# A recurrent attention layer with a token mixer behind it: k and r loaded four tokens to a partition, states kept as diagonal blocks, the last batch's V loaded whole, and a new order of steps

## The chip, the core and the metric

One core of a Trainium2 chip runs the whole program. The time is that of the device for one execution, in microseconds, as the median of several runs. Beside the runs there is one profiled execution with its trace: its span is the time from the first to the last instruction. The engines are TensorE (PE, with its weight loads PEld), VectorE (DVE), ScalarE (ACT), GpSimd (POOL) and SyncE (SP), which here only issues DMA transfers.

## The reference

Inputs r, k, v and w are float32 of the shape (4 batches, 8 heads, 768 tokens, 48 values); u is (8, 48). Each batch and head runs a recurrence over the tokens; the outcome of all heads side by side (384 values a token) then goes through a mixer over the tokens.

```python
for t in range(S):
    cur = np.einsum('bhd,bhe->bhde', u[None] * kt, vt)
    y[:, :, t] = np.einsum('bhd,bhde->bhe', rt, state + cur)
    state = wt[:, :, :, None] * state + np.einsum('bhd,bhe->bhde', kt, vt)
...
wq = x @ w_q                       # (tokens, 64)
wk = x @ w_k
W_tok = scale * np.einsum('bsd,btd->bst', wq, wk)
mixed = np.einsum('bst,btd->bsd', W_tok, x)
return np.maximum(mixed, 0.0) @ w_out
```

## The kernel before

The work is cut into 12 units of 256 tokens (three to a batch), each of two chunks of 128 tokens. For a unit, `unit` (L406) lays out these steps:

- Load w, k, r, v (`load`, L229): each partition takes two neighbouring tokens of every head, so a row is 96 floats (384 bytes), and all 128 partitions are filled by one transfer. In seven units (`DIRECT`, L339) V is loaded by `load_v` (L221) in four transfers of 64 partitions and 192-byte rows, which put the tokens into their order at once. In the other five V is put in order on PE by a permutation matrix (`f_v16` L565, `f_vp` L570) and copied out of PSUM (`f_vb` L580). There are four buffers for each of w, k, r and v.
- ACT takes the logarithm of w (lw, L466), POOL, ACT or DVE cast k and r to bf16 (`f_c16`, L472). PE sums the logarithms with a mask CM (`f_cw`, L485), ACT makes the exponentials en and ep (L497, L503). PE transposes k and r (`f_rawT`, L510). DVE or ACT copies kT (ks), DVE makes RT = rT x ep and qT = rT x ks, POOL or DVE makes KT = ks x en (L545). POOL makes ptm (L552), the decay over a chunk, by head.
- PE multiplies KT and RT (`f_A` L608, 64-row tiles), DVE masks it with US (AM, L618, 128x1024).
- PE transposes KT back (kb), ACT or DVE copies it with a scale (kd). The state: `f_sn` (L650) adds the old state through the identity (384 columns) and four products of 128 by 96 columns, each for a pair of heads, of which DVE keeps the diagonal blocks by a product with ptm, zero elsewhere (`f_sb` L664, SB of 384 columns).
- y: eight products with AM and four of the old state with RT (`f_y`, L673). DVE adds the bonus term Vd from POOL (X, L704).
- For the mixer PE transposes X (xt), a copy makes XT, PE makes wk and wq (`f_qk`, L728), a copy makes QK. When the three units of a batch are done: T (`f_T` L766, six products of 384 columns), TS, and for each unit mx, rl (relu, MX), fp (product with wo), os (copy) and a store. The order of tokens is undone in the operand of `f_mx` (L793).

Pieces of the last unit are cut in halves (`each`) to shorten the end. Every product is issued through `mm` (L181), so the profile has all of PE's work on that line.

The order on each engine is decided before the kernel is built. `Plan.add` records a step with its engine, length and a rank; `Plan.order` (L64) sorts each engine's queue by rank and walks through them with the buffers' ring sizes and PSUM's eight banks, issuing the step that can start first. `RANK` (L304) holds the ranks, `ENG` the engine for steps that may run on either of two. SyncE's queue is such a queue: loads and stores follow each other in it. The setup ahead of unit 0 (L245 to L293) clears buffers on DVE and builds masks on POOL; 42 products with a zero matrix (`warm`, L385) and nine at the start keep PE running.

Of the kernel before, what the change touches and what calls it, by code (L numbers as in the profile page):

```python
# [14 lines left out]
AX = mybir.AxisListType  # L15
# [9 lines left out]

class Plan:

    def __init__(self, kinds, switch):
        self.kinds = kinds
        self.switch = switch
        self.steps = []

    def add(self, eng, dur, rank, fn, after=(), fill=None, read=(), lag=100, mode=0,
            behind=None):
        s = dict(mode=mode, behind=behind, eng=eng, dur=dur, rank=rank, fn=fn, after=[a for a in after if a is not None],  # L40
                 fill=fill, lag=lag, n=len(self.steps), out=[])
        s["buf"] = None if fill is None else dict(readers=[])
        self.steps.append(s)
        for a in read:
            self.reads(s, a)
        return s

    def dma(self, issue, dur, rank, fn, after=(), fill=None, read=()):

        i = self.add("SP", issue, rank, fn, after, fill, read, lag=0)  # L50
        m = self.add("DQ", dur, 0, self.nothing, [i], lag=0)
        return i, self.add(f"L{m['n']}", 1950, 0, self.nothing, [m], lag=0)

    def nothing(self):
        pass

    def reads(self, s, a, own=False):

        if not own:
            s["after"].append(a)  # L60
        if a["buf"] is not None:
            a["buf"]["readers"].append(s)

    def order(self):  # L64
        never = 1 << 60
        queues = {e: [] for e in ("PE", "ACT", "DVE", "POOL", "SP")}
        for s in sorted(self.steps, key=lambda s: s["rank"]):
            if s["eng"] in queues:
                queues[s["eng"]].append(s)
            for a in s["after"]:  # L70
                a["out"].append(s)
        free = dict.fromkeys(queues, 0)
        free["DQ"] = 0
        place = dict.fromkeys(queues, 0)
        rings, owners, moved, done, mode = {}, [None] * 8, [], [], 0

        def clear(buf):

            if buf is None:
                return 0  # L80
            return max([x.get("end", never) for x in buf["readers"]], default=0)

        def start(s):

            if any("end" not in a for a in s["after"]):
                return never, None
            if s["behind"] is not None and "start" not in s["behind"]:
                return never, None
            t = max([free[s["eng"]]] + [a["end"] for a in s["after"]])
            if s["behind"] is not None:  # L90
                t = max(t, s["behind"]["start"])
            if s["eng"] == "SP" and len(moved) >= 3:
                t = max(t, moved[-3])
# [13 lines left out]
            if s["fill"] is not None:  # L107

                ring, size = rings.setdefault(s["fill"], []), self.kinds[s["fill"]]
                if len(ring) >= size:  # L110
                    t = max(t, clear(ring[-size]))
# [7 lines left out]
        while True:  # L119
# [7 lines left out]
            if at is not None:  # L127
                s["buf"]["bank"] = at
                for x in range(at[0], sum(at)):
                    owners[x] = s["buf"]  # L130
            elif s["fill"] is not None:
                rings[s["fill"]].append(s["buf"])
            change = e == "PE" and s["mode"] != mode
            if e == "PE":
                mode = s["mode"]
            run(s, t, s["dur"] + self.switch * change)
            if e == "SP":
                for m in s["out"]:
                    if m["eng"] == "DQ":
                        run(m, max(free["DQ"], s["end"]), m["dur"])  # L140
                        moved.append(free["DQ"])
                        for x in m["out"]:
                            if x["eng"].startswith("L"):
                                run(x, m["end"], x["dur"])
        assert len(done) == len(self.steps)
        return done


@with_exitstack
def kernel(  # L150
# [14 lines left out]
    C = 128  # L165
# [9 lines left out]
    HW = H * D2  # L175

    SHIFT = 25
    MU = -SHIFT * math.log(2.0) / C

    def mm(o, l, rr, start=True, stop=True, trans=False):  # L180
        nc.tensor.matmul(o, l, rr, start=start, stop=stop,  # L181
                         skip_group_check=True, is_transpose=trans)
# [4 lines left out]
    sm = ctx.enter_context(tc.tile_pool(name="sm", bufs=3))  # L187
    bt = ctx.enter_context(tc.tile_pool(name="bt", bufs=2))
# [6 lines left out]
    NB = 4  # L195
    WG = [const([C, HW], F32, f"wg{i}") for i in range(NB)]
    RG = [const([C, HW], F32, f"rg{i}") for i in range(NB)]
    KG = [const([C, HW], F32, f"kg{i}") for i in range(NB)]
    VG = [const([C, HW], F32, f"vg{i}") for i in range(NB)]
    NOS = 4  # L200
    OS = [const([C, 2 * DM], F32, f"os{i}") for i in range(NOS)]
    EW = 132

    KDS = [const([C, 1024], BF16, f"kd{i}") for i in range(2)]
    LW = [const([C, 2 * H * 64], BF16, f"lw{i}") for i in range(2)]
    R16 = [const([C, 2 * H * 64], BF16, f"r16{i}") for i in range(2)]
    K16 = [const([C, 2 * H * 64], BF16, f"k16{i}") for i in range(2)]
    QK = [const([C, NU * 384], BF16, f"qk{i}") for i in range(2)]
    TS = [const([C, DM], BF16, f"ts{i}") for i in range(2)]
    EP = [const([C, 8 * EW], BF16, f"ep{i}") for i in range(2)]  # L210

# [8 lines left out]

    def load_v(b, i, tl):  # L221

        for c in range(2):
            src = v[b, :, ds(i * U + c * C, C)].rearrange("h (q j) d -> j q h d", j=2)
            for j in range(2):
                nc.sync.dma_start(out=view(tl, c * DM, [[D, H], [1, D]], p0=64 * j, pn=64),  # L226
                                  in_=src[j])
# [6 lines left out]
    ID16 = const([C, C], BF16, "ID16")  # L234
    Z = const([C, 512], BF16, "Z")
    US = const([C, C], F32, "US")
    CM = const([C, 2 * C], BF16, "CM")
    PM = const([C, 2 * C], BF16, "PM")
    MB = const([C, 2], F32, "MB")
    pos0 = const([C, 1], mybir.dt.int32, "pos0")  # L240
    pos1 = const([C, 1], mybir.dt.int32, "pos1")
    gx = const([C, 1], F32, "gx")
    gv = const([C, 1], F32, "gv")

    nc.vector.memset(Z, 0.0)  # L245
    for _ in range(9):
        mm(PS[:, ds(0, 512)], Z[:, ds(0, C)], Z)
    nc.vector.memset(uT, 0.0)  # L248
    for hh in range(2):
        nc.scalar.dma_start(out=view(uT, hh, [[2, NP], [1, 1]], p0=hh * 64, pn=D),  # L250
                            in_=dataclasses.replace(u, offset=hh * D,
                                                    ap=[[1, D], [D2, NP], [1, 1]]))

    nc.vector.memset(CM, 1.0)
    nc.vector.memset(US, 1.0)
    nc.vector.memset(ID16, 0.0)
    nc.vector.memset(PM, 0.0)
    for t in LW:
        nc.vector.memset(t, 0.0)
    for t in TS:  # L260
        nc.vector.memset(t[64:128, :], 0.0)
    for t in EP:
        nc.vector.memset(view(t, 0, [[EW, 8], [1, 1]]), 1.0)
    for t in R16 + K16 + KDS:
        nc.vector.memset(t, 0.0)  # L265
    nc.vector.memset(MB, 0.0)
    nc.vector.memset(MB[0:D, 0:1], 2.0 ** -SHIFT)
    nc.vector.memset(MB[64:64 + D, 1:2], 2.0 ** -SHIFT)

    for j in range(2):  # L270
        nc.gpsimd.iota(pos0[ds(64 * j, 64), :], pattern=[[0, 1]], base=j, channel_multiplier=2)
        nc.gpsimd.iota(pos1[ds(64 * j, 64), :], pattern=[[0, 1]], base=j + 1,
                       channel_multiplier=2)
    nc.scalar.activation(gx, pos0, ACT.Exp, bias=0.0, scale=MU)
    nc.scalar.activation(gv, pos1, ACT.Exp, bias=0.0, scale=-MU)
    for c in range(2):
        for j in range(2):
            m = view(CM, j * C, [[64, 2], [1, 64]], p0=c * 64, pn=64)
            nc.gpsimd.affine_select(m, m, pattern=[[1, 2], [2, 64]], compare_op=ALU.is_ge,
                                    fill=0.0, base=-j, channel_multiplier=-2)  # L280
    for c in range(2):
        for j in range(2):
            m = PM[ds(c * 64, 64), ds(j * C + j * 64, 64)]
            nc.gpsimd.affine_select(m, m, pattern=[[1, 64]], compare_op=ALU.not_equal,
                                    fill=1.0, base=0, channel_multiplier=-1)
    nc.gpsimd.affine_select(ID16, ID16, pattern=[[1, C]], compare_op=ALU.not_equal, fill=1.0,
                            base=0, channel_multiplier=-1)
    for j in range(2):
        m = view(US, 0, [[64, 2], [1, 64]], p0=j * 64, pn=64)
# [627 lines left out]
```

## Time and profile before

| | |
|---|---|
| runs | 106.95, 106.95, 108.07 us; median 106.95 |
| profiled execution | span 105.2 us; the profile has no other time of it |
| granted TensorE clock | 1.000 |
| DMA | 24.62 MB, 61217 packets, 58896 of them under 512 B |
| loads w, k, r | 12 each, 384 KB, 5.3, 5.0, 5.1 us to landing |
| loads v | 5 of 384 KB, 5.0 us to landing; 28 of 96 KB, 3.7 us |
| AM on DVE | 24 x 1220 ns |
| KT on POOL | 8 whole, 2129 ns, 2 halves, 1154 ns |

Busy time of an engine is the time in which it has an instruction under way. For PE a product stays in the array much longer than the distance to the next one, so its busy time is not its load; the distance of the starts is. In the groups of the profile `out<-in` names the tiles, then come partitions x elements, the count, the busy time and the mean length of one, and the idle time ahead of it with what ended it. A row of the timeline or of the chain begins with its start and its length in microseconds; `SPq` is SyncE's queue, where a transfer's length is the time that the issue took.

### The profile page before, as it was taken

Reading aid. Unit: us, or ns where it says so; the run is one execution under the profiler, and the core shown is the slowest. Engines: PE = TensorE matmul, PEld = TensorE weight load, DVE = VectorE, ACT = ScalarE, POOL = GpSimd, SP = SyncE. Lnnn points to the kernel's source line nnn. Section 1 sums busy time; section 2 is a strip of 40 time slices with the busy share of each in tenths; the row PEclk is TensorE's granted clock in tenths of the full one; section 3 lists DMA queues with packets and bytes.
Section 4 is the critical chain, followed back from the end, with each engine's and each line's share of the span. In section 5 each row is a group of like instructions: output and inputs, shape, how many; then the busy total and the mean of one; then the engine's idle time right before and its main releaser. Section 6 shows DMA issues by size and latency. Waiting matters only on the chain.

```text
span 105.2 us, 3714 instructions
## 1 busy us (share of the span) xinstructions
PE 96.2 (91%) x1506; PEld 70.2 (67%) x1506; DVE 88.1 (84%) x138; ACT 79.9 (76%) x123; POOL 71.0 (67%) x92
## 2 busy tenths in 40 slices
PE   5969889997999998999997897779999999998995
PEld 2246566686887786968796775658697987856551
DVE  6898997898999999798999996786998889754740
ACT  4367778797989868997899959867898895954610
POOL 6600859599997996979979993968689699000000
DMA  1999999999999898989997969998997870033564
GB/s 28 298 324 325 325 323 270 238 297 175 312 316 264 148 272 230 288 172 310 325 311 142 213 123 269 350 289 209 288 255 143 303 307 18 0 153 150 199 243 160
DMA packets 61217, 24.62 MB, mean 234 GB/s; under 512 B 58896, under 2 KB 60048, under 8 KB 61200
## 3 DMA queue, kind: packets, MB, share of 16 engines
q1 hardware_dynamic: 60640, 24.19, 85.5%
q10 hardware_dynamic: 560, 0.20, 0.7%
q8 instruction: 11, 0.18, 0.7%
q14 instruction: 6, 0.05, 0.1%
HBM read 19.66 MB, written 4.72 MB: 232 GB/s over the span
## 4 chain that ended last, share of the span: by engine, by line
PE 51%; DVE 14%; DMA 13%; issue 7%; POOL 5%; ACT 4%; SPq 4%; DVEq 0%; ACTq 0%; POOLq 0%
PE PS L181 51%; DMA wg<-in_w_dram 7%; DMA kg<-in_k_dram 6%; SPq L226 3%; DVE SB L666 2%; DVE RT L536 2%; POOL KT L547 2%; DVE qT L529 2%; DVE KT L547 2%; POOL Vd L601 1%; ACT MX L381 1%; SPq L230 1%; ACT kd L373 1%; DVE X L707 1%; DVE kd L265 1%
## 5 line engine op out<-in xcount | busy, mean ns | idle before, releaser
L619 DVE TENSOR_TENSOR AM<-PS,US 128x1024 bf16<-128x1024 f32 x24 | 28.9, 1220 | 1.1 <-PE PS L181 0.7
L547 POOL TENSOR_TENSOR KT<-ks,en 128x1024 bf16<-128x1024 bf16 (+1 forms) x10 | 19.3, 1934 | 1.2 <-ACT en L498 0.6
L601 POOL TENSOR_TENSOR Vd<-VB,dd 128x768 bf16<-128x768 bf16 (+1 forms) x14 | 18.4, 1318 | 2.2 <-ACT dd L371 1.3
L181 PE MATMUL PS<-Z 128*128 128x512 bf16 x51 | 16.2, 424 | 1.5 <-DVE uT L248 1.2
L707 DVE SCALAR_TENSOR_TENSOR X<-PS,gx,Vd 128x768 bf16<-128x768 f32 (+1 forms) x13 | 12.3, 955 | 3.3 <-PE PS L181 2.8
L181 PEld LDWEIGHTS <-KT 48*128 48x128 bf16 (+1 forms) x272 | 10.7, 95 | 6.3 <-issue 3.8
L467 ACT ACTIVATE lw<-wg 128x768 bf16<-128x768 f32 x12 | 10.0, 846 | 5.5 <-DMA wg<-in_w_dram 5.1
L181 PE MATMUL PS<-wo,MX 128*128 128x384 bf16 x72 | 13.5, 326 | 0.1
L504 ACT ACTIVATE ep<-PS 128x1024 bf16<-128x1024 f32 (+1 forms) x14 | 12.7, 922 | 0.9 <-PE PS L181 0.9
L498 ACT ACTIVATE en<-PS 128x1024 bf16<-128x1024 f32 (+1 forms) x14 | 12.5, 904 | 0.5 <-issue 0.3
L666 DVE TENSOR_TENSOR SB<-PS,ptm 128x384 bf16<-128x384 f32 x20 | 11.1, 553 | 1.5 <-PE PS L181 1.3
L181 PE MATMUL PS<-RT,KT 48*128 48x128 bf16 x192 | 9.2, 217 | 1.4 <-POOL KT L547 0.5
L381 ACT ACTIVATE MX<-PS 128x768 bf16<-128x768 f32 (+1 forms) x12 | 8.7, 730 | 1.8 <-PE PS L181 1.7
L475 POOL CAST r<-rg 128x768 bf16<-128x768 f32 x10 | 8.7, 870 | 1.6 <-DMA rg<-in_r_dram 1.5
L475 POOL CAST k<-kg 128x768 bf16<-128x768 f32 x9 | 7.4, 825 | 3.3 <-DMA kg<-in_k_dram 2.0
L181 PE MATMUL PS<-ID,k 128*128 128x128 bf16 x96 | 7.4, 220 | 2.2 <-POOL k L475 1.4
L181 PEld LDWEIGHTS <-MX 128*128 128x128 bf16 x72 | 6.7, 98 | 3.9 <-issue 0.3
L373 ACT ACTIVATE kd<-PS,gv 128x384 bf16<-128x384 bf16 (+1 forms) x11 | 8.1, 740 | 1.4 <-PE PS L181 1.3
L181 PEld LDWEIGHTS <-Z 128*128 128x128 bf16 x51 | 5.0, 105 | 6.0 <-issue 2.3
L371 ACT COPY os<-PS 128x768 f32<-128x768 f32 (+1 forms) x10 | 7.1, 708 | 2.5 <-PE PS L181 2.2
L536 DVE TENSOR_TENSOR RT<-PS,ep 128x1024 bf16<-128x1024 bf16 (+1 forms) x14 | 8.4, 609 | 0.5 <-PE PS L181 0.2
L181 PE MATMUL PS<-CM,lw 64*128 64x128 bf16 x192 | 7.8, 223 | 1.1 <-ACT XT L371 0.7
(82 smaller groups left out, 211.4 us busy)
## 6 DMA issues: line engine op xcount, KB each, us to landing
wg<-in_w_dram SPq DMA_DIRECT2D x12, 384.0 KB, 5.3
kg<-in_k_dram SPq DMA_DIRECT2D x12, 384.0 KB, 5.0
rg<-in_r_dram SPq DMA_DIRECT2D x12, 384.0 KB, 5.1
out_dram<-os SPq DMA_DIRECT2D x9, 384.0 KB, 4.3
vg<-in_v_dram SPq DMA_DIRECT2D x28, 96.0 KB, 3.7
vg<-in_v_dram SPq DMA_DIRECT2D x5, 384.0 KB, 5.0
out_dram<-os SPq DMA_DIRECT2D x5, 192.0 KB, 2.0
wof<-in_moe_w_out_dram SPq DMA_DIRECT2D x1, 576.0 KB, 5.7
```

What stands on the lines that cost most here:

```text
L181: nc.tensor.matmul(o, l, rr, start=start, stop=stop, skip_group_check=True, is_transpose=trans)
L381: nc.scalar.activation(o, i, ACT.Relu)
L467: nc.scalar.activation(view(lw, 0, [[64, H], [512, 2], [1, D]]), view(wg, 0, [[D2, H], [D, 2], [1, D]]), ACT.Ln, bias=0.0, scale=math.exp( ...
L475: op(view(dst, 0, [[64, H], [512, 2], [1, D]]), view(src, 0, [[D2, H], [D, 2], [1, D]]))
L498: nc.scalar.activation(sb("en", [C, 1024])[:, cols(cs, 512)], t["cw"][:, cols(cs, 512)], ACT.Exp, bias=0.0, scale=-1.0)
L504: nc.scalar.activation(view(ep, cs[0] * NP * EW + 66, [[EW, NP * len(cs)], [-65, 2], [1, 64]]), t["cw"][:, cols(cs, 512)], ACT.Exp, bias=0 ...
L536: nc.vector.tensor_tensor(view(sb("RT", [C, 1024]), cs[0] * 512, [[C, n4], [64, 2], [1, 64]]), view(t["rT"], cs[0] * 512, [[C, n4], [64, 2 ...
L547: e.tensor_tensor(sb("KT", [C, 1024])[:, cols(cs, 512)], t["ks"][:, cols(cs, 512)], t["en"][:, cols(cs, 512)], ALU.mult)
L601: nc.gpsimd.tensor_tensor(sb("Vd", [C, 2 * DM])[:, cols(cs, DM)], t["VB"][:, cols(cs, DM)], view(t["dd"], cs[0] * H, [[1, len(cs) * H], [0 ...
L619: nc.vector.tensor_tensor(view(sb(f"AM{c}", [C, 1024]), 0, [[C, 8], [1, C]]), view(t[f"A{c}"], 0, [[C, 8], [1, C]]), view(US, 0, [[0, 8], ...
L666: nc.vector.tensor_tensor(view(x, 0, [[D, H], [1, D]]), view(t[f"sn{c}"], 0, [[D, H], [1, D]]), view(t["ptm"], c * 8, [[1, 8], [0, D]]), A ...
L707: nc.vector.scalar_tensor_tensor(view(X["t"], (2 * i + c0) * DM, [[DM, ncs], [1, DM]]), view(t["y"], c0 * 512, [[512, ncs], [1, DM]]), gx, ...
```

## The change

The file is rewritten around the same stages. What changes in the work:

- k and r: each partition takes four neighbouring tokens of four heads (rows of 768 bytes); heads 0 to 3 go to partitions 0 to 63, heads 4 to 7 to the others, by one transfer each (`load_runs`). A chunk's tokens so stand in four runs of 32, in place of two of 64; CM, US and PM follow, and rl undoes the order.
- V of batch 3 is loaded for the whole batch in eight transfers of 32 partitions with 192-byte rows (`load_whole`) and only cast by POOL; the nine units of the other batches take the way over PE and a copy to VB. No unit has `load_v`.
- The state is kept as diagonal blocks: SB has 192 columns, the two heads of a pair at partitions 0 and 64. kd has a window of 128 columns for each head; `f_sn` does eight products of 48 columns, and the old state goes in through a scaled identity of 192 columns. `f_yi` multiplies RT and the old state in 64-row tiles, eight products for a unit's chunk, in two groups with a drain between them (13 drains in all). ptm is gone: POOL copies 31 columns of ep in each block (`f_ew`), and DVE reads the decay from ep.
- T is built for both chunks at once in the two halves of the array's columns.
- Setup clears only the pads of lw, k16, r16 and kd. POOL casts k of unit 0, DVE r.
- The ranks, the choice of engines (`ALT`) and the warm-up products (11, and nine at the start) are new. Stores of 1536-byte rows; every load stands ahead of every store in SyncE's queue.

The core of the diff:

```diff
-    def load_v(b, i, tl):
-        for c in range(2):
-            src = v[b, :, ds(i * U + c * C, C)].rearrange("h (q j) d -> j q h d", j=2)
-            for j in range(2):
-                nc.sync.dma_start(out=view(tl, c * DM, [[D, H], [1, D]], p0=64 * j, pn=64),
-                                  in_=src[j])
+    def load_runs(b, i, hb, tl, ap):
+        nc.sync.dma_start(
+            out=view(tl, 0, [[4 * D, NP], [1, 4 * D]], p0=64 * hb, pn=64),
+            in_=dataclasses.replace(ap, offset=((b * H + NP * hb) * S + i * U) * D,
+                                    ap=[[4 * D, 64], [S * D, NP], [1, 4 * D]]))
+    def load_whole(b, q, tl):
+        n_ = H // 2 * NCH
+        for j in range(4):
+            nc.sync.dma_start(
+                out=view(tl, q * n_ * D, [[D, n_], [1, D]], p0=32 * j, pn=32),
+                in_=dataclasses.replace(v, offset=(b * H * S + j) * D + q * n_ * C * D,
+                                        ap=[[4 * D, 32], [C * D, n_], [1, D]]))
...
-    for t in R16 + K16 + KDS:
-        nc.vector.memset(t, 0.0)
+        for x in (tiles["lw"][0], tiles["k16"][0], tiles["r16"][0]):
+            nc.vector.memset(view(x, D, pads), 0.0)
...
+        for x in tiles["kd"]:
+            nc.vector.memset(x[:, ds(0, 64)], 0.0)
+            nc.vector.memset(view(x, 64 + D, [[128, 16], [1, 128 - D]]), 0.0)
...
-            def f_ptm(cs=cs, n4=n4):
-                nc.gpsimd.tensor_tensor(
-                    view(sb("ptm", [C, 16], F32), cs[0] * 8, [[2, n4], [1, 2]]),
-                    view(ep, cs[0] * NP * EW + 64, [[EW, n4], [0, 2]]),
-                    view(MB, 0, [[0, n4], [1, 2]]), ALU.mult)
+            def f_ew(e, cs=cs):
+                o = cs[0] * NP * EW
+                nc.gpsimd.tensor_copy(view(ep.tile, o + 1, [[EW, NP * len(cs)], [1, 31]]),
+                                      view(ep.tile, o + C, [[EW, NP * len(cs)], [1, 31]]))
...
-                    if old is not None:
-                        mm(x[:, ds(0, DM)], ID16, old.tile, start=True, stop=False)
-                    for hp in range(NP):
-                        mm(x[:, ds(hp * D2, D2)], KDS[n % 2][:, ds((c * NP + hp) * C, C)],
-                           t["VB"][:, ds(c * DM + hp * D2, D2)],
+                if old is not None:
+                    mm(x[:, ds(0, NP * D)], IDU, old.tile, start=True, stop=False)
+                for hp in range(NP):
+                    for hh in range(2):
+                        h = 2 * hp + hh
+                        mm(x[:, ds(hp * D, D)],
+                           kd.tile[:, ds(64 + (c * H + h) * 128 - 64 * hh, 128)],
+                           VB.tile[:, ds(c * DM + h * D, D)],
...
-                    for hp in range(NP):
-                        mm(y[:, ds(c * 512 + hp * D2, D2)], t["RT"][:, ds((c * NP + hp) * C, C)],
-                           old.tile[:, ds(hp * D2, D2)], start=False, stop=True)
+                if not first:
+                    nc.tensor.drain()
+                for hp in range(NP):
+                    for c, hh in side:
+                        mm(of(c, 2 * hp + hh), RT.tile[ds(hh * 64, D), ds((c * NP + hp) * C, C)],
+                           olds[c].tile[ds(hh * 64, D), ds(hp * D, D)],
+                           start=(first and hp == 0), stop=False)
...
-                    mm(batch["T"][:, ds(0, DM)], batch["QK"][:, ds(ii * 384 + c * DH, C)],
-                       X["t"][:, ds(gi_ * DM, DM)], start=(gi_ == 0), stop=(gi_ == NCH - 1))
+                mm(at(T)[ds(c * DH, DH), ds(0, DM)], QK.tile[:, ds(ii * QS + U + c * DH, DH)],
+                   X.tile[:, ds(gi * DM, DM)], start=(gi < 2), stop=(gi >= NCH - 2))
...
-                    relu(e, view(t[f"MX{ii}"], cs[0] * C, [[U, NK], [1, w_]]),
-                         view(t[f"mx{ii}"], cs[0] * C, [[U, NK], [1, w_]]))
+                    e, view(MX.tile, cs[0] * C, [[U * C // w_, NK * w_ // C], [4, 32], [1, 4]]),
+                    view(at(mx), cs[0] * C, [[U * C // w_, NK * w_ // C], [1, 32], [32, 4]])),
...
-                    issue, land = plan.dma(
-                        500, 580 * len(cs), STEP * n + OFF["st"] + 6 * ii, f_st(nc.sync),
-                        [go.by[c] for c in cs])
+                    plan.dma(("st", m, cs[0]), 400, 480 * len(cs), f_st, [oss[cs]], reads=[o])
```

How many instructions of each kind stand on each engine, before and after, as the prediction uses them:

| engine | step | before | after |
|---|---|---|---|
| SP | transfers issued | 86 | 94 |
| DVE | ks, XT (768), dd | 6, 4, 3 | 7, 2, 6 |
| DVE | kd, 768 and 384 columns | 2, 0 | 3, 3 |
| DVE | os; MX; QK (384) | 5; 3; 1 | 1; 5; 2 |
| ACT | VB; k and r casts; XT (768) | 5; 3; 7 | 9; 0; 9 |
| ACT | kd; os | 11; 10 | 7; 14 |
| POOL | k and r casts; V and VB casts | 19; 12 | 23; 12 |
| POOL | KT, whole and half | 8, 2 | 7, 3 |
| POOL | ptm; ep copy | 14; 0 | 0; 14 |
| PE | state products; products of RT and state | 80; 80 | 160; 160 |
| PE | V permuted; products with zeros | 20; 51 | 36; 20 |
| PE | changes between ways of tiling the array | 57 | 90 |

## The prediction

> **What bounds the kernel now.** I read the page first, for the share of each engine, then the windows of ten microseconds, for the stage in which each is full, then SyncE's timeline, for the price of a transfer, then the chain that ended last.
>
> The page, its first lines and the two DMA rows (40 slices of 2.6 us):
>
> ```profile
> span 105.2 us, 3714 instructions
> PE 96.2 (91%) x1506; PEld 70.2 (67%) x1506; DVE 88.1 (84%) x138; ACT 79.9 (76%) x123; POOL 71.0 (67%) x92
> ...
> DMA  1999999999999898989997969998997870033564
> GB/s 28 298 324 325 325 323 270 238 297 175 312 316 264 148 272 230 288 172 310 325 311 142 213 123 269 350 289 209 288 255 143 303 307 18 0 153 150 199 243 160
> ```
>
> The DMA engines are full until slice 33 (87 us) and nearly idle afterwards. Inside the full stretch the rate drops from 325 to 123-175 GB/s in six places: there the split V loads run.
>
> The windows (the columns are PE, PEld, DVE, ACT, POOL busy, the clock, the DMA share, GB/s):
>
> ```profile
> 20.00:30.00 10.00, 9.46 (x188) 7.50 (x184) 9.10 (x13) 9.39 (x15) 8.93 (x9) 1.00 1.09 270
> 50.00:60.00 10.00, 9.04 (x189) 7.81 (x187) 9.64 (x13) 9.26 (x13) 9.36 (x10) 1.00 0.98 247
> 60.00:70.00 10.00, 8.38 (x147) 6.20 (x143) 8.17 (x10) 7.90 (x13) 7.14 (x9) 1.00 0.99 260
> 80.00:90.00 10.00, 10.00 (x186) 7.92 (x185) 8.88 (x13) 8.06 (x16) 8.54 (x10) 1.00 0.54 184
> ```
>
> Two limits lie close together. DVE runs at 91% from 10 to 90 us (72.7 of 80), with 9.64 as its best window; where the DMA holds it up, at 60-70, all four engines fall together. PE's busy time says little, since a 128-column matmul stays 220 ns but the next starts 56 ns later; counting starts, PE needs 67 of the 80 us, and 97% of 70-90, where work delayed by late inputs has piled up.
>
> SyncE's timeline (issue start, length):
>
> ```profile
> 8.05 1.15 SPq L230 DMA_DIRECT2D kg<-in_k_dram  x1
> 9.24 1.11 SPq L230 DMA_DIRECT2D wg<-in_w_dram  x1
> ...
> 57.51 3.93 SPq L226 DMA_DIRECT2D vg<-in_v_dram  x4
> ...
> 77.22 2.66 SPq L226 DMA_DIRECT2D vg<-in_v_dram  x4
> 81.30 20.64 SPq L838 DMA_DIRECT2D out_dram<-os  x12
> ```
>
> With the queue full an ordinary load costs 1.2 us (393 KB, 384-byte rows), a split V 2.66 to 4.48, mean 3.54. Sum: 41 x 1.2 + 7 x 3.54 + weights 2.1 + two stores 2.0 = 78.1 of the 81.0 us from the first packets to the last landing (82.3, in the trace).
>
> The chain, its end:
>
> ```profile
> 63.30 6.31 DMA kg<-in_k_dram
> 69.60 0.05 issue
> 69.66 0.84 POOL k L475
> 70.49 0.05 issue
> 70.54 22.65 PE PS L181 x390
> ```
>
> A k load lets POOL cast, and from there PE runs without a hole. So: DMA first, DVE and PE just behind it.
>
> **The change part by part.** Counts are from the instruction orders of both kernels, durations from the groups of the profile.
>
> *Loads.* w stays 12 x 1.2 = 14.4. Nine V's stay whole: 10.8. k and r become 24 pairs of 64-partition transfers with 768-byte rows. No row shows such a transfer. Cheapest: the 1536-byte half stores at the end land 0.5 us apart, 1.0 a pair. Dearest: a half costs what a whole one does, 2.4. I take 1.15, a little under the 384-byte row, as to row length it lies between that and the stores. V of the last batch is 1.18 MB in eight pieces of 192-byte rows: at the issue row of such a piece (0.63) 5.0, by bytes at the split V's price 10.6; I take 8. Weights 2.1. Sum 14.4 + 10.8 + 27.6 + 8 + 2.1 = 62.9, against 78.1; all stores come after the loads. The inputs could be in 15 us sooner. I count this as nothing by itself, for the loads cannot run more than four units ahead (four buffers), and the engines are right behind: it removes the DMA waits, and the engines decide. SyncE issues 94 instead of 86 transfers of 0.33 to 0.63 us, at most 59 us of its time: hidden.
> [...]
>
> *DVE.* The state is kept in diagonal blocks, so SB has 192 columns: DVE copies of 128 and 384 f32 columns take 282 and 558 ns, so 192 take 351; 20 x (553 - 351) = -4.04. The new step order moves work: ks one more (+0.69), XT two fewer (-1.10), kd one wide and three halves more (+1.68), dd three more (+0.51), KT +0.03. Together -2.2 ahead of the last AM. Behind it os -3.0, MX +1.5, QK +0.3, all beside waits of the tail.
>
> *POOL.* Four more k and r casts (+3.4), V and VB casts 0, KT -1.0, ptm gone (-3.2). New is a copy of 31 columns in each block of ep (L520): 248 columns, between UB's 8 (187 ns) and wk's 192 (337 ns, 0.82 ns a column), so 0.39, halves 0.28: 10 x 0.39 + 4 x 0.28 = +5.0; at the rate of KT (1.9 ns a column) 8. Together +4.2. RT waits for this copy, so behind POOL's queue stand RT, A and AM; POOL's queue is the new place for a stall.
>
> *ACT.* VB +3.2, casts -2.5, kd -2.7, XT +1.6, os +2.6, MX -1.3, ks -1.0, the rest -0.8: -0.9. Nothing.
>
> *PE.* By distance of starts in the trace: identity onto the state 16 x (163 - 83) = -1.3; T in two column halves at once -2.0 (0 if they do not pair); block products 160 x 25 - 80 x 42 = +0.6; V permuted in four more units +1.3; RT times state 160 at 12.5 (paired, as A's) to 25 against 80 x 42: -1.4 to +0.6, taken -0.4. Changing the tiling of the array costs 95 ns (last of A to the next: 148 instead of 53); there are 90 changes instead of 57: +3.1. Thirteen drains, 0 to 206 ns (one matmul's stay), at 0.1: +1.3. Sum +2.6, bounds +0.3 to +7.0. It lies beside DVE and POOL except in 70-97 us; there it is covered only if earlier inputs unload that stretch.
>
> *Start.* DVE's eight 128x512 memsets (485 ns each) shrink to six of 128 elements (165) and two of 640 (0.6). The first k cast goes to POOL, behind 8 iotas and 13 selects (0.29), ready near 5.6; r is cast by DVE when it lands, 7.0. Then ks, qT, KT, RT, ks take 0.56 (r), 0.69, 0.68, 0.43, 0.42, 0.69 and 0.42 (second half of RT): first AM at 10.9 instead of 11.99: -1.1, bounds -1.5 and +0.5 (if v, now eleventh in the queue, holds VB).
>
> *Middle.* From 10 us to the last AM (90.2) DVE had 72.9 of 80.2; now 70.7. At the same share 77.8 (-2.4), at 95%, just under its best windows, 74.4 (-5.8). POOL had 67.5 from 10.6 to its last Vd at 89.5; now 70.0, since 1.65 of the casts moves into the empty start. At the best window's 94% that takes 74.5: -4.4; at 89%, 0. I take -3.4, midway between DVE's old share and POOL's cap. The waits that must vanish for it are there: after the start ACT waits 2.8 us for wg, POOL 4.9 for k, r and VB.
>
> *Tail.* From the last AM to the end 15 us of single steps; rl reads with a stride, stores have 1536-byte rows: 0, bounds -0.5 and +1.
>
> Sum: 105.2 - 1.1 - 3.4 = 100.7 of the profiled execution. The runs (106.95, 106.95, 108.07) have a median 1.75 above its span; I keep that: 102.4.
>
> **The rivals.**
> 1. *DMA was the whole limit.* Speaks for it: 97% full, PE piled up behind it. Then DVE runs at 95% throughout: -5.8 - 1.1, so 100.0. Against: three other engines would need 93% at once.
> 2. *PE takes over.* Changes and drains (+4.4) fall into the full stretch at 70-97, and T does not pair (+2.0): 2.6 + 2.0 = 4.6 against the forecast, 107.0. Against: DMA's delay is what filled it.
> 3. *POOL becomes the bound (slower).* Place: POOL's queue, ep copies ahead of RT. If POOL keeps its old share of 85.6%, 70.0 takes 81.8 instead of 78.9: +2.9, less 1.1: 108.8. It decides from where POOL cannot exceed 88%. Against: it reached 94%.
> 4. *The halves do not pay (slower).* A pair at 2.4: loads 95.5, last landing 97 instead of 82.3: 121. It decides from 1.9 a pair ((81.0 - 35.3) / 24). Against: split V pieces of half the bytes, on 64 partitions, already land 0.2 to 0.4 us apart where they queue up.
>
> **How the numbers follow.** Forecast 0.58 (own range 100.8 to 104.8: start and tail bounds), rival 1 0.22, rival 2 0.09, rival 3 0.07, rival 4 0.04. About 1% is what a measurement here can tell from no change, that is 105.9 to 108.0: faster 0.80, same 0.09, slower 0.11. The range 99.0 to 107.0 leaves out rivals 3 and 4 and a sliver under rival 1.
>
> **What would show it.** Right: the last load lands before 75, the GB/s row loses its drops except in one place, SB near 351 ns, the wide DVE windows at 93% or more, first AM near 10.9, waits for DMA small. Wrong: DMA full past 80 (rival 4); RT or KT waiting for POOL, POOL at 95% (rival 3); PE without holes from 60 on (rival 2). Were the ep copy above 0.6 us or a change of PE's tiling above 0.15, the forecast would be too low.

## The result and the profile after

The changed kernel took 119.27 us (median of 120.2, 118.33, 118.26 and 121.66) beside 107.23 for the kernel before on the same chip: a ratio of 1.100 [1.092, 1.109], slower by a tenth, where 102.4 and faster was forecast. Some executions ran slower than the others of their kernel, here those of 120.2 and 121.66; the ratios, here and below, compare the others alone, so they can differ from the ratio of the medians. The profiled execution took 120.2 with a span of 118.5, 1.9 us more than the two quickest runs (116.6 each). Its granted clock was 0.97 on the mean, 1.000 before.

The page's first lines and the two DMA rows (40 slices of 2.96 us):

```profile
span 118.5 us, 4048 instructions
...
DMA  1999999999999999979989999989993315303592
GB/s 29 260 233 258 250 275 239 246 239 238 224 296 264 214 220 213 231 201 242 262 239 269 243 222 204 175 168 152 242 291 132 135 63 211 134 1 132 204 368 101
```

Before, the rate stood at 325 GB/s and dropped in six places. Now the drops are gone but for one (152, V of the last batch), as forecast, but so are the 325: up to that place the row stands at 201 to 296, with the engines just as full. The loads (18.9 MB) ran from 1.9 to 81.8 us before and run from 2.3 to 88.2 now.

The windows (PE, PEld, DVE, ACT, POOL busy, the clock, the DMA share, GB/s):

```profile
20.00:30.00 10.00, 7.52 (x155) 6.45 (x153) 7.01 (x12) 7.58 (x10) 7.36 (x10) 0.83 1.05 237
50.00:60.00 10.00, 8.73 (x164) 6.80 (x162) 8.32 (x13) 7.91 (x13) 7.76 (x9) 1.00 1.05 242
60.00:70.00 10.00, 9.05 (x205) 7.19 (x199) 8.44 (x12) 8.60 (x13) 8.46 (x8) 1.00 1.10 239
70.00:80.00 10.00, 7.26 (x142) 6.11 (x136) 6.29 (x10) 6.09 (x8) 7.89 (x9) 0.86 1.05 188
80.00:90.00 10.00, 9.79 (x201) 8.24 (x199) 8.40 (x13) 8.83 (x13) 10.00 (x11) 0.97 1.01 239
```

Read them across: in 20 to 30 us all four engines are at 70 to 76%, where DVE had 9.10 and ACT 9.39 before. When all fall together and the last columns are full, none of them is the limit; the transfers are. The clock of 0.83, 0.86 and 0.97 in three of these windows takes at most 1.7 + 1.4 + 0.3 = 3.4 us from PE, which is too little for the loss of 12. The waits say the same (engine, what it waited for, total, times, longest):

```profile
ACT lw L470 <- DMA wg<-in_w_dram: 11.6, 7, 3.4
POOL k L480 <- DMA kg<-in_k_dram: 7.0, 7, 2.5
DVE SB L678 <- PE PS L243: 6.7, 7, 1.6
...
POOL r L480 <- DMA rg<-in_r_dram: 5.2, 5, 2.1
```

The same two waits before:

```profile
ACT lw L467 <- DMA wg<-in_w_dram: 5.1, 4, 2.3
POOL k L475 <- DMA kg<-in_k_dram: 2.0, 3, 1.0
```

These were to become small and have more than doubled. Note that w, whose transfer was not changed, is hit hardest: it stands in the same queue.

SyncE's timeline, near its end (issue start, length):

```profile
65.96 0.55 SPq L295 DMA_DIRECT2D wg<-in_w_dram  x1
66.57 1.96 SPq L301 DMA_DIRECT2D rg<-in_r_dram  x1
68.58 2.29 SPq L301 DMA_DIRECT2D kg<-in_k_dram  x3
...
71.58 8.43 SPq L309 DMA_DIRECT2D vw<-in_v_dram  x8
...
83.93 0.60 SPq L301 DMA_DIRECT2D rg<-in_r_dram  x1
```

V of the last batch takes 8.4 us of the queue (8 was taken). The last r is issued at 83.9, and the chain that ended last has a k in it:

```profile
68.58 7.27 DMA kg<-in_k_dram
75.88 0.70 POOL k L480
76.63 4.35 PE PS L243 x69
...
101.72 11.21 PE PS L243 x119
112.96 0.48 ACT os L395
```

As before, a late k lets POOL cast, and from there PE runs nearly to the end. The k lands 6.2 us later than in the chain of before (75.9, there 69.6); the other 7 us of the 13.3 between the spans come behind it, where more work is left.

### The profile page after: what moved, and what is told of

Its sections match the earlier page's. It is cut to its first block, busy times and chain, and to the rows that moved or that the text cites. A ratio compares the mean times of both kernels' runs of the same rounds, so it can differ in the third digit from the quotient of the medians.

```text
span 118.5 us, 4048 instructions
## 1 busy us (share of the span) xinstructions
PE 94.8 (80%) x1650; PEld 71.2 (60%) x1651; DVE 82.0 (69%) x140; ACT 80.7 (68%) x120; POOL 76.0 (64%) x102
## 4 chain that ended last, share of the span: by engine, by line
PE 39%; DMA 34%; SPq 11%; POOL 4%; issue 3%; ACT 3%; DVE 2%; POOLq 0%; ACTq 0%
PE PS L243 39%; DMA vg<-in_v_dram 14%; DMA kg<-in_k_dram 10%; DMA wg<-in_w_dram 10%; SPq L301 10%; POOL KT L563 2%; SPq L295 2%; POOL k L480 1%; ACT ks L395 1%; ACT os L395 1%; DVE X L736 1%; ACT lw L470 1%; POOL r L480 1%; DVE AM L632 1%; DVE qT L546 1%
## 5 line engine op out<-in xcount | busy, mean ns | idle before, releaser
L563 POOL TENSOR_TENSOR KT<-ks,en 128x1024 bf16<-128x1024 bf16 (+1 forms) x10 | 18.4, 1836 | 0.0
L480 POOL CAST k<-kg 128x768 bf16<-128x768 f32 x12 | 9.8, 825 | 7.0 <-DMA kg<-in_k_dram 7.0
L243 PE MATMUL PS<-wo,MX 128*128 128x384 bf16 x72 | 13.3, 326 | 0.0
L580 POOL CAST v<-vg 128x768 bf16<-128x768 f32 x9 | 7.5, 830 | 7.1 <-PE PS L243 4.4
L395 ACT COPY os<-PS 128x768 f32<-128x768 f32 (+1 forms) x14 | 9.5, 686 | 3.7 <-PE PS L243 3.6
L678 DVE TENSOR_TENSOR SB<-PS,ep 128x192 bf16<-128x192 f32 x20 | 7.0, 352 | 6.9 <-PE PS L243 6.7
L243 PE MATMUL PS<-ID,r 128*128 128x128 bf16 x96 | 7.6, 224 | 3.5 <-POOL r L480 2.8
L243 PE MATMUL PS<-RT,KT 48*128 48x128 bf16 x192 | 9.7, 221 | 0.7 <-DVE qT L546 0.5
L243 PEld LDWEIGHTS <-k 128*128 128x128 bf16 x96 | 5.8, 101 | 6.6 <-POOL k L480 6.4
L407 ACT ACTIVATE MX<-PS 128x768 bf16<-128x768 f32 (+1 forms) x10 | 7.3, 748 | 2.4 <-PE PS L243 1.8
```

Source lines behind the costliest of these rows:

```text
L243: return nc.tensor.matmul(o, l, rr, start=start, stop=stop, skip_group_check=True, is_transpose=trans)
L395: nc.scalar.copy(o, i)
L480: op(view(o.tile, 0, [[64, NP], [256, 4], [1, D]]), view(g[src].tile, 0, [[4 * D, NP], [D, 4], [1, D]]))
L563: x.tensor_tensor(KT.tile[:, cols], ks.tile[:, cols], en.tile[:, cols], ALU.mult)
```

## The experiments

**The theory** after this result: rival 4 happened, and what makes it happen is where the halves lie. A transfer into 64 neighbouring partitions is written more slowly than one into all 128, whatever its row length. **The rivals**: 768-byte rows are slow; two transfers in place of one cost a fixed price each; the new order of steps or a fuller engine is to blame and the loads only show it.

### The loads alone

Nothing is computed; eight tiles of 393 KB in each form, then a DVE copy that waits for them all.

```diff
+        for load in (wide, wide_halves, runs, runs_other, runs_full, split_v, quarters, wide):
+            for t in range(8):
+                load(x, b, i, t)
+            nc.vector.tensor_copy(T, view(G, 0, [[HW, 8]]))
```

> A kernel of loads alone (its output is not the reference's: nothing is computed), eight tiles of 393 KB in each form, one form after the other. Theory (a transfer into 64 neighbouring partitions is written at about two thirds of the rate): whole 128-partition loads 1.2 us a tile; the same 384-byte rows cut into two halves of 64 neighbouring partitions 1.7; the changed kernel's 768-byte halves 1.7; the same halves on every other partition 1.15; 768-byte rows on all 128 partitions 1.15; V in pieces of 32 partitions slower than its split into 64. Rival (the 768-byte rows, or what they read of memory, are slow): the 384-byte halves stay at 1.2, and all three forms with 768-byte rows take 1.7. Rival (the order of the steps, not the loads): all forms but those with 192-byte rows take 1.1 to 1.2.

DVE's timeline; the last bracket of each copy is the time that it waited, that is the stage:

```profile
19.22 0.17 DVE L110 COPY T<-G 128x8 f32<-128x8 f32 x1 [11.94 <-DMA G<-in_w_dram]
35.54 0.17 DVE L110 COPY T<-G 128x8 f32<-128x8 f32 x1 [16.15 <-DMA G<-in_w_dram]
51.49 0.17 DVE L110 COPY T<-G 128x8 f32<-128x8 f32 x1 [15.78 <-DMA G<-in_w_dram]
65.65 0.17 DVE L110 COPY T<-G 128x8 f32<-128x8 f32 x1 [13.99 <-DMA G<-in_w_dram]
78.38 0.17 DVE L110 COPY T<-G 128x8 f32<-128x8 f32 x1 [12.56 <-DMA G<-in_w_dram]
101.17 0.17 DVE L110 COPY T<-G 128x8 f32<-128x8 f32 x1 [22.62 <-DMA G<-in_w_dram]
120.46 0.17 DVE L110 COPY T<-G 128x8 f32<-128x8 f32 x1 [19.11 <-DMA G<-in_w_dram]
```

In order: whole 384-byte rows 11.94 us; 64 neighbours with 384-byte rows 16.15; 64 neighbours with 768-byte rows 15.78; 768-byte rows on every other partition 13.99; on all 128 partitions 12.56; V split into 64 partitions 22.62, and in pieces of 32 partitions 19.11. From the first packet to the last of a stage the first five are 302, 224, 233, 260 and 276 GB/s, and a tile in two halves of neighbours costs 14.04 / 8 = 1.75 or 13.52 / 8 = 1.69 us, where the prediction had 1.15. A whole tile costs 10.40 / 8 = 1.30 here, and a pair on every other partition or on all 128 costs 1.51 or 1.43, so these too are dearer than the 1.15 that I expected for them. Rows of 384 bytes and of 768 are nearly equally slow on 64 neighbours (14.04 and 13.52), so row length falls as a cause; the same 768-byte halves on every other partition are 1.8 us quicker, so it is the place. The packets show it too: a 384-byte packet takes 22 ns in the whole loads and 32 (median) in the halves; a 768-byte one 36 on all or on every other partition and 54 on neighbours.

The split V pieces of before (192-byte rows on 64 partitions) gave 22.62 us for the stage, but here the issue set their pace (0.68 us from one to the next, four to a tile). A piece has 98 KB, which at that pace is 145 GB/s, about what the rate fell to in the drops of before (123 to 175). So the row that the prediction held against rival 4, pieces landing 0.2 to 0.4 us apart, showed landings that bunch and no rate, and did not bear on it. Pieces of 32 partitions, expected to be slower than these, were quicker; with 0.53 us from one issue to the next they too stood near the pace of the issue.

### The halves alone, in the kernel before

```diff
+        if any(tl is x for x in KG + RG):
+            for hb in range(2):
+                nc.sync.dma_start(
+                    out=view(tl, 0, [[D2, H], [1, D2]], p0=64 * hb, pn=64),
+                    in_=ap[b, :, ds(i * U + C * hb, C)].rearrange("h (p j) d -> p h (j d)", j=2))
+            return
```

> The kernel before with k and r loaded in two transfers of 64 neighbouring partitions each, rows of 384 bytes as before. Theory: 24 pairs at 1.7 instead of 1.2 us, +12, so 117 to 120. Rivals (rows, order): 107, within 1%.

Measured 115.74 (114.89 to 119.14), ratio 1.079 [1.064, 1.094]. A little less than the 117 to 120 expected. Every value lands where it did before; only the loads of k and r are cut in two, so no new step order and no fuller engine can be blamed. Its GB/s row, beside which the 325 of before should be held:

```profile
GB/s 59 259 265 259 245 284 221 236 242 265 203 246 249 240 200 228 243 222 180 288 238 285 143 200 151 253 293 267 261 208 218 137 394 167 6 142 139 142 243 180
```

### Two transfers, but of all 128 partitions

```diff
+                nc.sync.dma_start(
+                    out=view(tl, NP * hb * D2, [[D2, NP], [1, D2]]),
+                    in_=ap[b, ds(NP * hb, NP), ds(i * U, U)].rearrange(
+                        "h (p j) d -> p h (j d)", j=2))
```

> The kernel before, with k and r each loaded by two transfers, but each of all 128 partitions and four of the eight heads (384-byte rows as before). The output is the reference's. My theory (what costs is that a transfer goes into 64 neighbouring partitions only): a pair costs what one whole load did, 1.2 us, the rate stays at 320 to 325 GB/s in its best slices, and the time is that of before, 106.5 to 108.5. Rival A (it is the number of transfers, each with a fixed price on the wire): the same 115 to 117 as with the two halves, 115.7. Rival B (two transfers are even better spread): 104 to 106.

Measured 109.62 (108.18 to 110.27) beside 107.96, ratio 1.021 [1.002, 1.040]. The number of transfers is not the main cause: it accounts for about 2% (0.2 to 4.0 by the interval) where the halves cost 8%. My theory had it as free, 106.5 to 108.5; by this it probably is not. The row starts at the old rate, and 384-byte packets take 23.0 ns on the mean (22.8 before, 26.6 with the halves):

```profile
GB/s 47 288 324 322 324 322 244 266 269 96 249 291 160 238 204 314 227 206 226 290 295 244 135 239 185 253 347 250 272 209 224 219 328 119 0 148 145 175 244 166
```

### The change without halves of neighbours

Two forms. In the first, each of the two transfers fills all 128 partitions with two heads (it reads other tokens for half of them, so its outcome is not the reference's):

```diff
-            out=view(tl, 0, [[4 * D, NP], [1, 4 * D]], p0=64 * hb, pn=64),
+            out=view(tl, 2 * hb * 4 * D, [[4 * D, NP // 2], [1, 4 * D]]),
```

> The changed kernel, but each of the two transfers for k and r fills all 128 partitions with two heads (768-byte rows, same bytes and same number of transfers; the upper half of the partitions gets the tokens of the next unit instead of heads 4 to 7, so the output is not the reference's). Theory: 24 pairs back to 1.15, loads done by 75 us, 101 to 105. Rivals (rows, order): 117 to 120 as the changed kernel.

In the second, heads 0 to 3 go to the even partitions and 4 to 7 to the odd ones, and the matrix by which PE transposes k and r puts them back; everything is computed:

```diff
-            out=view(tl, 0, [[4 * D, NP], [1, 4 * D]], p0=64 * hb, pn=64),
+            out=every_other(view(tl, 0, [[4 * D, NP], [1, 4 * D]], p0=hb, pn=127)),
...
-                           src.tile[:, ds(j * 256 + hs * 128, 128)], ID16, trans=True)
+                           src.tile[:, ds(j * 256 + hs * 128, 128)], IDP, trans=True)
```

> The changed kernel with heads 0 to 3 on the even and heads 4 to 7 on the odd partitions, and a permutation in place of the identity in the transposes of k and r. Theory, if what counts is which partitions a transfer fills and not how many: 101 to 105 as with all 128. If it is the number of 64 partitions: 117 to 120. Rivals (rows, order): 117 to 120.

Measured: 104.36 (103.73 to 105.17), ratio 0.974 [0.965, 0.982], and 105.73 (105.36 to 106.80), ratio 0.988 [0.979, 0.996]. Both forms have the changed kernel's number of bytes and of transfers and its rows of 768 bytes; with another place to land they take 14.9 and 13.5 us off 119.27. The first is within the 101 to 105 expected, the second 0.7 above it. The rest of the change does pay: the second form, which computes everything, beats both kernels, the kernel before by 1.2%, hardly more than the 1% that can be told here. GB/s of the first, then of the second:

```profile
GB/s 51 288 347 326 329 322 300 335 288 291 331 328 334 273 287 307 246 291 239 326 330 330 294 127 178 234 325 312 15 0 157 72 240 57 98 4 221 266 364 67
```

```profile
GB/s 26 288 296 299 306 305 283 294 306 312 317 317 288 265 236 248 281 264 266 287 279 332 335 288 142 188 144 242 338 88 150 38 274 24 129 6 205 263 364 69
```

The last load's packets come at 71.3 and 76.1 us, in place of 88.2. "Before 75" was the forecast: it holds in the first form and is missed by 1.1 us in the second.

### What limits once the loads are quick

The first form gained 2.7% where 4.3% was forecast. Its windows at 50 to 80 us:

```profile
50.00:60.00 10.00, 9.79 (x216) 7.88 (x217) 9.40 (x14) 9.32 (x13) 10.00 (x9) 1.00 1.12 313
60.00:70.00 10.00, 9.89 (x214) 8.19 (x213) 9.38 (x15) 9.39 (x14) 10.00 (x12) 1.00 0.97 220
70.00:80.00 10.00, 9.79 (x209) 8.11 (x207) 8.82 (x15) 9.13 (x14) 8.66 (x11) 1.00 0.33 119
```

POOL is full at 50 to 70 (rival 3) and PE has hardly a hole (rival 2). So each was unloaded in the second form: POOL by leaving out the copy in ep, PE by leaving out the products of RT and the old state.

```diff
-            x = add(("ew", n, cs[0]), {"P": 110 + 124 * len(cs)}, f_ew, [x], ep)
+            x = add(("ew", n, cs[0]), {"P": 0}, None, [x], ep)
```

> The kernel with heads on every other partition (105.7), without the copy of 31 columns of ep on POOL (it leaves out f_ew; the decays of the first run of 32 in each chunk are wrong, so the output is not the reference's). It takes 5.7 us of work off POOL and one step off the way to RT. Theory POOL (rival 3 of the prediction: POOL's queue is the bound once the loads are quick, it shows 10.00 of 10 in 50 to 70 us): 103 to 104, and POOL falls to 9.2 there. Theory PE (rival 2: tiling changes and drains fill PE from 40 us on, where its demand and the changes come to 96%): 105.3 to 106, PE unchanged at 9.8 to 9.9.

```diff
-            x = add(("yi", n, *side[0]), {"E": 54 * len(side) + 60 * bool(yis[cs[0]])}, f_yi,
+            x = add(("yi", n, *side[0]), {"E": 0}, None,
```

> The kernel with heads on every other partition (105.7), without the products of RT and the old state and without their 13 drains (it leaves out the old state's part of y, so the output is not the reference's). PE loses 4.6 us of bursts and up to 3 us of changes of the tiling; no other engine loses or gains an instruction. Theory PE: 101.5 to 103.5, PE has holes again between 40 and 90 us. Theory POOL: 105 to 106.

Measured: without the copy 105.49 (103.96 to 106.51), ratio 0.983 [0.975, 0.991]; without the products 103.67 (103.46 to 104.08), ratio 0.975 [0.965, 0.985]. Both beside the 0.988 [0.979, 0.996] of the second form. 5.7 us less on POOL bring 0.4%, which the intervals do not tell from nothing, so POOL is not the bound although its windows read 10.00 (they still read 9.83 without the copy, where 9.2 was expected). Less work on PE brings about 1.3%, less than the 2 to 4% that I expected, and the intervals overlap. The windows without the products:

```profile
50.00:60.00 10.00, 9.53 (x189) 7.24 (x188) 9.67 (x14) 9.10 (x15) 10.00 (x9) 1.00 1.04 295
60.00:70.00 10.00, 10.00 (x206) 8.30 (x206) 9.35 (x16) 9.69 (x14) 9.79 (x10) 1.00 0.97 182
```

PE still reads 9.5 to 10.0 with less to do, which is how a busy column misleads: a product's stay fills the gaps (in the kernel before a 128-column product stays 220 ns, and the next starts 56 ns after it). The four engines are at 91% or more here. The chains that ended last show what follows (the second form, then without the products):

```profile
PE 56%; issue 1%; ACT 1%; ACTq 0%
PE 33%; SPq 21%; DMA 13%; POOL 9%; issue 8%; DVE 5%; ACT 5%; POOLq 0%; ACTq 0%; DVEq 0%
```

In the second form the chain can be followed back to 40 us, and it is PE nearly throughout. Without the products PE's share falls, and between 41 and 72 us loads of k and V with their issue, and POOL, take its place. So PE holds the second form from 40 us on, with the loads and POOL close behind it; this is read from the chains. No run makes the loads quicker still, and the second form's waits for them are not small: from 10 us on POOL waits 3.8 us for k and ACT 3.1 for w (2.0 and 2.7 before; in the first form 0 and 1.1).

### V of the last batch, more or less of it

To price the whole load of V, it was done for two batches, and for none, in the second form; the steps that this adds had to be put into the written order by hand.

```diff
-    WHOLE = (3,)
+    WHOLE = (2, 3)
```

> The kernel with heads on every other partition (105.7), and V loaded whole for the batches 2 and 3 instead of batch 3 alone; the transfers take the places of V of units 5 to 7 in SyncE's queue. The output is the reference's. PE loses three permutations of V with their changes of the tiling (3 x (0.42 + 0.19) = 1.8 us), ACT three copies of 0.8 (2.4); SyncE gets eight pieces (8 us) for three loads (3.6). Theory PE (from 40 us on PE is the limit and inputs are early by then): 103.5 to 105. Rival (the loads still limit the middle, as 48 halves and the pieces leave no slack before 60 us): 106.5 to 109, with waits of POOL for V of batch 2.

```diff
-    WHOLE = (3,)
+    WHOLE = ()
```

> The kernel with heads on every other partition (105.7), and V of batch 3 loaded like the others (three whole loads, permuted on PE, copied by ACT) instead of whole in eight pieces. The output is the reference's. PE gains 1.8 us, ACT 2.4, and the loads shrink by about 4.4 us. Theory PE: 107 to 108.5, slower than with V whole, so that part of the change pays by itself. Rival (the loads still limit): 102 to 105, and the whole load of V would be the next loss.

Measured 115.83, ratio 1.082 [1.070, 1.095], and 112.68, ratio 1.059 [1.052, 1.067]. Both are far above either expectation, and both have one hole in which the engines stand for 2.4 to 6.4 us: at 50 to 60 us with two batches (DVE 3.11 of 10), at 70 to 80 with none (DVE 5.33). The first also didn't keep to its own text: the pieces were put ahead of k of units 7 and 8, not where V had stood. Each was then moved (with a larger move of V of units 9 to 11 the steps wait for each other in a circle, so there is no time of it):

```diff
 ranks of the two pieces of V of batch 2 in SyncE's queue (k of units 7 and 8 has 46 to 49)
-    43.5, 45.5
+    50, 51
```

> As whole_two, which took 115.8: there the pieces of V of batch 2 stood ahead of k of units 7 and 8 in SyncE's queue, a k landed 4 us late and all engines had a hole at 50 to 58 us. Here they stand where V of units 6 and 7 stood, behind these k. The output is the reference's. Theory PE: without that hole 104 to 106. Rival (the loads still limit: the eight pieces are 4.4 us more of transfers ahead of 60 us, wherever they stand): 108 to 113, with POOL waiting for V of batch 2 or for the k and r behind it.

```diff
 ranks of V of units 9, 10 and 11: its load in SyncE's queue, its cast in POOL's
-    58.5, 66, 67; 63, 66, 69
+    57.5, 61, 65.5; 60.5, 64.5, 67.5
```

> As whole_none (112.7), with the casts of V of units 9 to 11 two or three steps earlier in POOL's queue and their loads one or two earlier in SyncE's. The output is the reference's. If the hole at 71 to 75 us, where PE waited 2.9 us for the cast of V, goes: 107 to 109 by the theory that PE limits (1.8 us more of PE, 2.4 of ACT), 102 to 105 by the rival that the loads limit. If it only moves: 110 or more, and V whole can't be priced by taking it out of this order.

Measured 110.42 beside 109.11, ratio 1.005 [0.997, 1.014], and 115.21 beside 107.59, ratio 1.078 [1.065, 1.091]. With two whole batches the wait moved to V itself:

```profile
POOL VB L583 <- DMA vw<-in_v_dram: 4.7, 1, 4.7
```

That speaks for the rival in the expectation: before 60 us the second form has no slack in its loads for eight more small pieces. With none the hole stays (DVE 4.56 of 10 at 70 to 80; PE waits 3.1 us for a cast of V, ACT 3.4 for PE). By what was said ahead of that run, V whole can't be priced by taking it out of this order. It stays open. In three of the four profiled executions the clock is lower in or after the hole (two batches: 0.67 at 50 to 60 us; moved: 0.53 at 60 to 70; none, moved: 0.83 at 70 to 80), so part of these times may be the clock's.

### The place alone, once more

```diff
+    def runs_two(x, b, i, t):          # 3 and 7
+        half(nc.sync, x, b, i, t, 0, 0)
+        half(nc.scalar, x, b, i, t, 1, 64)
+    def lower(x, b, i, t):             # 4
+        half(nc.sync, x, b, i, t, 0, 0)
+    def middle(x, b, i, t):            # 5
+        half(nc.sync, x, b, i, t, 0, 32)
```

> Loads alone (nothing is computed, the output is a copy of loaded tiles and not the reference's), eight 393 KB tiles in each form, then a copy that waits for them: 1 whole 384-byte rows, 2 pairs of 64-partition halves (768-byte rows) all from SyncE, 3 the same with the upper half issued by ACT, so that the two halves stand in two queues, 4 eight lower halves alone (half the bytes), 5 eight halves on partitions 32 to 95, 6 whole loads alternating between the two queues, 7 as 3, 8 as 2. [...] Rival (a transfer of 64 partitions is slow by itself, wherever it lies): 3 and 7 like 2, and 5 like 4, 6.8 to 7.2. Rival (one queue is the limit, not the half): 6 beats 1 by as much as 3 beats 2.

The rates inside the stages, once each is under way (the last column is GB/s; PE is not used, so the columns are DVE, POOL, clock, DMA share, GB/s):

```profile
26.00:30.00 4.00, 0.00 (x0) 0.00 (x0) 1.00 1.11 233
38.00:39.00 1.00, 0.00 (x0) 0.00 (x0) 1.00 1.05 307
...
43.00:44.00 1.00, 0.00 (x0) 0.00 (x0) 1.00 1.10 234
...
48.00:49.00 1.00, 0.00 (x0) 0.00 (x0) 1.00 1.11 233
...
56.00:60.00 4.00, 0.00 (x0) 0.00 (x0) 1.00 1.13 196
65.00:69.00 4.00, 0.00 (x0) 0.00 (x0) 1.00 0.90 275
75.00:80.00 5.00, 0.00 (x0) 0.00 (x0) 1.00 1.17 325
```

Pairs from one queue 233 GB/s; lower halves alone 196; halves of the same size on partitions 32 to 95 275, with packets back at 36 ns and the engines not full (0.90; the issues, 0.61 us each, are near the pace); whole loads, from two queues in turn, 325. So a transfer of 64 partitions is not slow by itself: it is slow on 0 to 63 and quick on 32 to 95; the theory's "64 neighbouring partitions" was too wide. That the place decides is the theory's side. From first to last packet the difference is smaller: 7.75 us for the lower halves and 6.65 for the middle ones, where the rival had 6.8 to 7.2 for both.

The two queues (stages 3 and 7) took 13.1 and 13.2 us from first to last packet against 13.8 for stage 2: hardly quicker, as the rival had it. My own estimate, at best the 10.4 of the whole loads in the first run of loads alone, did not hold. Inside the stage the rate swings: 307 GB/s in one window, 234 in another. Counting the trace's packets by queue in stretches of one microsecond: 196 from one queue and 202 from the other gave 306 GB/s with packets at 44 ns; 226 and 80 gave 235 at 58 ns. Equal parts of both queues alone don't make it quick: at 48 to 49 us equal parts, 151 and 152, gave 233 too. What makes the rate swing is not shown. The rival with one queue as the limit falls: eight whole loads took 10.6 us from first to last packet from one queue and from two.

## Why the prediction was wrong

**The failed step** is the term "k and r become 24 pairs ... I take 1.15". The loads alone give 1.69 to 1.75 us a pair. And that is not all of it: the whole loads in the same queue are stretched too (384-byte packets 28.5 ns on the mean in the changed kernel, 22.8 before), so 21 x 1.2 = 25.2 became about 25.2 x 28.5 / 22.8 = 31.5, an estimate. With 24 x 1.7 = 40.8, V 8.4 and weights 2.1 the sum is 82.8, where the prediction had 62.9; the loads took 85.9 in the trace. Rival 4, "the halves do not pay", had the right place and the right sign, and a chance of 0.04. Its point of decision, 1.9 a pair, was too high, because it let the halves slow nothing but themselves. Its 121 came close by luck: it put the last landing at 97 us (88.9 measured) and left 23 us of work behind it, as before (29.6 measured). Its load sum of 95.5 also takes V at 10.6; with the 8 of the forecast it is 92.9.

Why the price was wrong: a new form of transfer was placed by row length, between the 384-byte rows and the 1536-byte stores, both of which fill all 128 partitions, and the place of the halves was left out of the choice, though the bound at 2.4 had been written down. The sentence on the split V pieces that weighed against it came from transfers paced by their issue.

The runs give the row that was wanted: 196 GB/s on partitions 0 to 63, 325 on all 128, 275 on 32 to 95 and 260 on every other (the last two with the issue near that pace). Two halves of neighbours from one queue ran at 224 to 233 GB/s, and took 1.30 to 1.35 times the time of whole loads in the same run.

Point by point:
- *Loads.* Wrong, as above. V of the last batch 8.4 (8 taken) and the last landing before 75 without the halves (71.3) were right, the last in the first form alone. The GB/s row lost its drops, but at a lower level.
- *DVE.* SB 352 ns (351 forecast). Right.
- *POOL.* The copy in ep takes 393 ns whole (0.39) but 336 in halves (0.28). Its removal brings next to nothing: rival 3 did not happen.
- *PE.* T pairs, as assumed: its products start 75.8 ns apart on the mean, 162.5 before, 24 x 0.087 = 2.1 (2.0 taken). RT times state comes every 16 to 18 ns (12.5 to 25 allowed).
- *Start.* First AM at 13.07 us in the changed kernel, 11.54 in the first form (10.9 forecast, 11.99 before): -0.45 where -1.1 was taken.
- *Middle.* In the first form, from the first AM to the last 76.0 us, before 78.2: -2.3, where -3.4 was taken.
- *Tail.* 16.0 us from the last AM to the end in all three versions of the changed kernel, 14.9 before: +1.0, the upper bound of the step, taken at 0. The sum of these three, -1.7, is the -1.7 between the spans 105.2 and 103.5.
- *Range.* The forecast's own range, 100.8 to 104.8, does not follow from the start and tail bounds named for it; they give 101.5 to 105.0.

So without the halves the forecast would still have been 2.8 us too low by the profiled execution (-1.7 where -4.5 was taken), and 2.0 by the median, 104.36; the steps are of the right kind, each too hopeful. That the changed kernel lost 12 us and the kernel before only 8 with halves goes with another number: from the last load's packets to the end it is 30.3 us in the changed kernel, 32.2 in the first form, and 23.3 before (23.1 before with halves). The new order leaves more work behind the last load, and so may be more sensitive to late loads; this is read from the traces and wasn't tried by itself.

## What to carry to other kernels

When a change alters a transfer's shape, price it by how many partitions it fills and which ones, before its row length: two halves on partitions 0 to 63 and 64 to 127 cost 1.30 to 1.35 times a whole load here, the same bytes on every other partition 1.16 times, and two heads on all 128 1.10 times. On 32 to 95, 64 partitions ran at 275 GB/s where 0 to 63 ran at 196. A slow transfer also stretches its neighbours in the queue (384-byte packets 28.5 ns in place of 22.8), so a price per transfer understates the loss. A bound that no row excludes deserves more than a chance of 0.04.

## What the runs showed that I had not expected

- Lower halves alone (196 GB/s) are slower than pairs of lower and upper (233), and in the second microsecond of a stage they still run at 254 and 280; why the start is quicker is not shown.
- SyncE's issue of a transfer of 64 partitions with four rows each takes 0.61 us (0.66 from one to the next), that of 128 partitions with two rows 0.47 (0.51, 1.03 a pair).
- An engine that reads 10.00 in two windows (POOL) could lose 5.7 us of work, and the time fell by 0.4%, within the noise.
- A few steps moved in a written order opened holes of 2.4 to 6.4 us in the engines, and the runs became 5 to 10 us longer, more than what they were meant to price.
